# Softmax reciprocals by way of a scratch row in device memory: attention and two MLPs on one core

## The chip, the cores and the metric

The kernel runs on one core of a Trainium2 chip. The metric is the time of one execution in device microseconds. The kernel before takes 557.91 us (median of 3 runs, 557.77 to 558.45).

## What is computed

Attention over 2 batches of 8 heads, 576 tokens, head size 64, all in float32; q and k are rotated first. Two MLPs follow on the 1152 x 512 result, each 512 to 2048 to 512, with the activations h*tanh(softplus(h)) and h*sigmoid(1.702 h).

```
scores = scale * matmul(q_rot, k_rot^T);  scores -= max(scores)
attn = exp(scores);  attn = attn / (sum(attn) + 1e-9);  y = matmul(attn, v)
x = y as (1152, 512)
x = mish(x @ w_in1) @ w_out1;  out = gelu_sigmoid(x @ w_in2) @ w_out2
```

## The kernel before, in words

Work goes by pairs of heads, 8 pairs in all. For each pair the 1152 query rows (576 of each head) are cut into nine tiles of 128 rows: tile n is even for the first head and odd for the second, and tile 8 holds the last 64 rows of both heads. For every tile TensorE makes the scores (`s_mm`, L256), VectorE takes the row maximum (`s_max`, L267), ScalarE the exponential (`s_exp`, L282), which also leaves the row sums in column n of a small tile `sums`. The exponentials are turned so that keys lie on the partitions: tiles 0 to 3 as fp16 parts through a DMA transpose (`p_turn`, L368), tiles 4 to 8 on TensorE (`e_turn`, L327; `rest_turn`, L353 to L357). Then they are multiplied with v into the one bank `pvps` (`pv_mm`), in two groups: g = 0 for tiles 0 to 3 (L408, 256 columns) and g = 1 for tiles 4 to 8 (L400, 320 columns). `pv_end` (L440) multiplies the sums over v with the reciprocals `rb` and splits the result into the two parts of x.

The result of a group has head and channel on 128 partitions and queries along the row, whereas the softmax sums have queries on the partitions. The steps r_* bring the reciprocals into the first form, once for each group: ScalarE adds a small constant (`r_prep`, L374), VectorE takes the reciprocal (`r_inv`, L378), ScalarE mostly widens each of four columns to 64 (`r_wide`, at L295 in the helper `copy`), in group 1 one engine scales a 128 x 64 identity by the fifth column (`r_rest`, L384 or L386), TensorE transposes two 128 x 128 blocks, plus one matmul of 64 columns in group 1 (`r_mm`, L424 and L426), and ScalarE copies the result out of PSUM, in group 0 with the scale of v (`r_copy`, L430).

The instruction order of all engines in the attention part is written by a planner, the class `Plan`. It plays the work as a list schedule with a cost for each step, takes the ready step with the lowest rank first (table `RANK`, one number for each kind of step, plus 1 for each tile of progress), and puts tiny matmuls on idle data (`keep_clock`, L680) where its play leaves TensorE idle. Buffers limit it: the PSUM bank with tag "m" serves one step at a time, `pvps` one group at a time, and three score tiles share the rest. After the last pair, work units of the first MLP (L571) are placed between the parts of the last group of attention. SP issues loads, DMA transposes and stores in order.

The MLP part that follows runs on TensorE with weights that VectorE and ScalarE split into two parts each. The result is stored at L1143 by row tiles of 128; where the row order of attention changes within a tile, the store is cut in two.

Of the kernel before, what the change touches and what calls it, by code (L numbers as in the profile page):

```python
# [22 lines left out]
def kernel(  # L23
# [34 lines left out]
    wp = ctx.enter_context(tc.tile_pool(name="wp", bufs=3))  # L58
    stages = {}
# [21 lines left out]
    def bank(name):  # L81
        return pm.tile([128, 512], F32, tag="m", name=name)
# [19 lines left out]
    P2 = [att.tile([128, 2, 2, KB * 128], F16, name=f"p2_{i}", bufs=1) for i in range(2)]  # L102
    x = xp.tile([128, 2, KD, TOK], F32R, tag="x", name="x")
# [159 lines left out]

    def s_max(st):
# [10 lines left out]
    def s_exp(p, n, st, nm):  # L275

        if p not in sums:
            sums[p] = att.tile([128, 9], F32, tag="sums", name="sums")
        if (p, n // 2) not in ebuf:
            name, w, bufs = ("e", 2, 3) if n < 8 else ("er", 1, 1)  # L280
            ebuf[p, n // 2] = att.tile([128, w, S], F32, tag=name, name=name, bufs=bufs)
        ACT.activation(  # L282
            out=ebuf[p, n // 2][:, n % 2, :].rearrange("p (g s) -> p g s", g=2),
            in_=st[:, :, 0:HALF], func=AF.Exp,
            bias=nm, scale=SCALE, accum_out=sums[p][:, n:n + 1],
        )
# [36 lines left out]
    COL = (0, 128, 0, 192)  # L323
# [16 lines left out]
    def e_out(p, c, ps, h, eng):  # L340
        t = pt_tile(p, 1)
        if c < 4:
            copy(eng, t[:, h, :, COL[c]:COL[c] + 128], ps[:, h].rearrange("k (b q) -> k b q", b=4))
        else:
            copy(eng, t[:, :, :, 128:192], ps.rearrange("k (b h q) -> k h b q", b=4, h=2))

    def rest_turn(p):


        ps = bank("eps")  # L350
        for c in (2, 3):
            b = slice(COL[c], COL[c] + 128)
            PE.transpose(ps[:, b], ebuf[p, c][:, 1, S - 128:S], ident)  # L353
            PE.transpose(ps[0:64, b], ebuf[p, c][:, 0, MAIN:S], ident)
        e = ebuf[p, 4][:, 0]
        PE.matmul(out=ps[:, 128:192], lhsT=e[:, S - 128:S], rhs=ident[:, 64:128], start=True, stop=True)
        PE.matmul(out=ps[0:64, 128:192], lhsT=e[:, MAIN:S], rhs=ident[:, 0:64], start=True, stop=True)  # L357
        return ps[:, 0:GW[1]]
# [11 lines left out]
    def r_prep(p, g):  # L370

        n = 4 + g
        t = rcs[p, g] = att.tile([128, 16], F32, tag="rc", name="rc")
        ACT.activation(out=t[:, 0:n], in_=sums[p][:, 4 * g:4 * g + n], func=AF.Copy, bias=1e-9 * PSC)  # L374

    def r_inv(p, g):
        n, t = 4 + g, rcs[p, g]
        DVE.reciprocal(out=t[:, 8:8 + n], in_=t[:, 0:n])  # L378
        return t

    def r_rest(p, t, eng):
        rr = rrs[p, 3] = att.tile([128, 64], F32, tag="rrr", name="rrr")
        if eng is ACT:
            ACT.activation(out=rr, in_=pair_id, func=AF.Copy, scale=t[:, 12:13])  # L384
        else:
            eng.tensor_scalar(rr, pair_id, t[:, 12:13], None, op0=ALU.mult)  # L386
# [26 lines left out]
    rbs, rcs = {}, {}  # L413

    def r_wide(p, g, eng):
        rr = rrs[p, 2 * g] = att.tile([128, 4, 64], F32, tag="rr", name="rr", bufs=1)
        copy(eng, rr, rcs.pop((p, g))[:, 8:12].unsqueeze(2).to_broadcast([128, 4, 64]))

    def r_mm(p, g, ps):

        rr = rrs.pop((p, 2 * g))
        for c in range(2):
            c0 = COL[2 * g + c]
            PE.transpose(ps[:, c0:c0 + 128], rr[:, 2 * c:2 * c + 2, :].rearrange("p a d -> p (a d)"), ident)  # L424
        if g:
            PE.matmul(out=ps[:, 128:192], lhsT=block, rhs=rrs.pop((p, 3)), start=True, stop=True)  # L426

    def r_copy(p, g, ps):
        rb = rbs[p, g] = att.tile([128, GW[g]], F32, tag=f"rb{g}", name=f"rb{g}")
        ACT.activation(out=rb, in_=ps, func=AF.Copy, scale=1.0 if g else vs[p][:, 1:2])  # L430

    def pv_end(p, g):
        W, ps, rb = GW[g], pv.pop((p, g)), rbs.pop((p, g))
        del PT[p, g]
        c0 = S * (p // NPAIR) + 256 * g
# [3 lines left out]
        def norm():  # L439
            DVE.tensor_tensor(out=xf[:, 0:W], in0=ps[:, 0:W], in1=rb[:, 0:W], op=ALU.mult)  # L440
# [242 lines left out]
    class Plan:  # L683
# [6 lines left out]
            er=1, p2=2, pt0=2, pt1=2, sums=2, rc=2, rr=1, rrr=2, rb0=2, rb1=2, xf=2, vs=2, vh=2,  # L690
# [167 lines left out]
        "xl": 7061.6, "rr ACT": 8301.4, "rr DVE": 6481.1, "rr": 5509.1, "rope": 8017.6, "rope POOL": 5814.7,  # L858
        "turn": 5193.8, "load w": 6242.4, "w": 9567.2, "w POOL": 7235.3, "u": 5436.8,
# [59 lines left out]
    def plan_pair(p):  # L919
# [33 lines left out]
        for at, n in enumerate(TILES[p]):  # L953
# [41 lines left out]
            holds=[("rawv", p // 2), ("vh", p)])  # L995
        for gr in range(2):
            t = base + 4 * gr
            k = 2 * p + gr
            add("ACT", 0.095, (t, "rc"), lambda gr=gr: r_prep(p, gr),
                needs=[("e", p, c) for c in ((0, 1), (2, 3, 4))[gr]], makes=("rs", p, gr),  # L1000
                holds=[("sums", p), ("rc", k)])
            add("DVE", 0.105, (t, "rc"), lambda gr=gr: d.update({("rc", gr): r_inv(p, gr)}),
                needs=[("rs", p, gr)], makes=("rc", p, gr), holds=[("rc", k)])
            add(None, dict(ACT=0.305, DVE=0.33, POOL=0.6), (t, "rw"), lambda eng, gr=gr: r_wide(p, gr, eng),
                needs=[("rc", p, gr)], makes=("rw", p, gr), holds=[("rc", k), ("rr", k)])
            if gr:
                add(None, dict(POOL=0.4, ACT=0.24, DVE=0.12), (t, "rr"), lambda eng: r_rest(p, d["rc", 1], eng),
                    needs=[("rc", p, gr)], makes=("rr", p, gr), holds=[("rc", k), ("rrr", p)])

            def spread(gr=gr):  # L1010
                d["r", gr] = bank("rps")[:, 0:GW[gr]]
                r_mm(p, gr, d["r", gr])
            where = ("m", ("r", k))
            add("PE", 0.216 + 0.31 * gr, (t, "rm"), spread, needs=[("rw", p, gr), (("vs", p), ("rr", p, gr))[gr]], makes=("rm", p, gr),
                holds=[where, ("rr", k)] + [("rrr", p)] * gr, work=256 + 64 * gr)
            add("ACT", 0.356 + 0.053 * gr, (t, "rb"), lambda gr=gr: r_copy(p, gr, d["r", gr]),
                needs=[("rm", p, gr)], makes=("rb", p, gr), holds=[where, (f"rb{gr}", p)] + [("vs", p // 2)] * (1 - gr))
# [8 lines left out]
            def norm(gr=gr):  # L1026
                d["end", gr] = pv_end(p, gr)
                d["end", gr][0]()
            add("DVE", 0.335 + 0.067 * gr, (t, "xf"), norm, needs=[("pv", p, gr, i), ("rb", p, gr)], makes=("xf", p, gr),
                holds=[("pv", k + 1), (f"rb{gr}", p), ("xf", k)])  # L1030
# [17 lines left out]
    for t in raw_v:  # L1048
        POOL.memset(t[64:128, :, :, 4, :], 1e-27)
    for t in P2:  # L1050
        DVE.memset(t[..., S:KB * 128], 0.0)
# [139 lines left out]
```

## Time and profile before

| | |
|---|---|
| median of 3 runs | 557.91 us |
| profiled execution | 558.24 us, span 556.5 us |
| TensorE matmul busy | 548.4 us (99%) |
| TensorE weight load busy | 495.6 us (89%) |
| VectorE busy | 342.6 us (62%) |
| ScalarE busy | 266.6 us (48%) |
| GpSimd busy | 83.6 us (15%) |
| granted TensorE clock | full in all slices |

The shares are means over two unlike parts: attention up to about 150 us and the MLPs behind it. Matmuls overlap each other, and their ends are modelled, so the matmul row of TensorE shows time in which it had matmuls under way. The chain of waits follows the work that ended last back to the start; the windows view gives busy time by stage.

### The profile page before, as it was taken

To read this page: it belongs to the slowest core of one execution; us is meant where nothing else is said; L and a number is where in the kernel's file an instruction comes from. 1 tells how busy PE (TensorE), PEld (TensorE's weight loads), DVE (VectorE), ACT (ScalarE), POOL (GpSimd) and SP (SyncE) were. 2 spreads that over 40 slices of the span, in tenths; PEclk is the share of its full clock that TensorE was granted. 3 is DMA by queue.
4 is the path that set the end of the run, shared out by engine and by line. 5 is a ranking of instruction groups with operands and counts; after the bars stand their busy time and mean duration, and the time that the engine had idled before them with its cause. 6 is when DMAs were issued, how large, how long until landed. Compare 5 with 4: busy or idle time off the path is not lost.

```text
span 556.5 us, 9033 instructions
## 1 busy us (share of the span) xinstructions
PE 548.4 (99%) x3571; PEld 495.6 (89%) x3571; DVE 342.6 (62%) x691; ACT 266.6 (48%) x578; POOL 83.6 (15%) x83
## 2 busy tenths in 40 slices
PE   8999999999999999999999999999999999999996
PEld 7887777777779999999999999999988889998885
DVE  6898989899718875355886557766520437820020
ACT  2887888988618651222865122275511226741000
POOL 2696775442200000000000000000000000000000
PEclk9999999999999999999999999999999999999999
DMA  7666585653504435134433322423220124200032
GB/s 210 141 134 133 125 199 113 93 128 88 136 1 139 132 109 152 40 116 121 141 118 111 114 75 77 122 73 109 78 74 0 45 82 140 76 1 1 0 114 57
DMA packets 81034, 54.52 MB, mean 98 GB/s; under 512 B 46816, under 2 KB 77792, under 8 KB 80992
## 3 DMA queue, kind: packets, MB, share of 16 engines
q1 hardware_dynamic: 80704, 53.62, 36.3%
q8 instruction: 28, 0.46, 0.4%
q10 hardware_dynamic: 288, 0.33, 0.2%
q14 instruction: 14, 0.11, 0.1%
HBM read 41.09 MB, written 2.36 MB: 78 GB/s over the span
## 4 chain that ended last, share of the span: by engine, by line
PE 95%; DVE 3%; DMA 1%; issue 1%; SPq 0%; DVEq 0%
PE h L571 32%; PE acc L638 16%; PE acc L652 16%; PE st L256 7%; PE pvps L400 5%; PE pvps L571 4%; PE st L327 2%; PE pvps L408 2%; PE pvps L638 2%; PE tps L227 2%; PE pvps L652 2%; DVE spill L267 1%; PE rps L424 1%; PE pvps L680 1%; DMA rest<-in_k_dram 1%; PE eps L327 1%
## 5 line engine op out<-in xcount | busy, mean ns | idle before, releaser
L571 PE MATMUL h<-x,whl 128*128 128x384 f32 x1008 | 179.2, 335 | 0.0
L571 PEld LDWEIGHTS h<-x,whl 128*128 128x128 f32 x1008 | 174.9, 188 | 2.7 <-issue 2.5
L502 DVE TENSOR_TENSOR whl<-wf,whl 128x512 fp32r<-128x512 f32 x62 | 42.9, 691 | 96.1 <-ACT whl L501 96.1
L652 PE MATMUL acc<-whl,g 128*128 128x512 f32 x384 | 88.9, 389 | 0.0
L638 PE MATMUL acc<-g,whl 128*128 128x384 f32 x504 | 88.6, 334 | 0.0
L638 PEld LDWEIGHTS acc<-g,whl 128*128 128x128 f32 x504 | 87.5, 188 | 0.0
L652 PEld LDWEIGHTS acc<-whl,g 128*128 128x128 f32 x384 | 72.0, 188 | 14.9
L608 DVE TENSOR_TENSOR g<-t,g 128x384 fp32r<-128x384 f32 x96 | 53.0, 553 | 27.2 <-ACT g L618 27.2
L501 ACT ACTIVATE whl<-wf 128x512 fp32r<-128x512 f32 x64 | 40.2, 628 | 60.1 <-DVE wf L520 40.8
L267 DVE CUSTOM_DVE_ANT_1 spill<-st,shift 128x576 f16<-128x576 f32 x72 | 54.2, 753 | 9.3 <-PE st L256 4.8
L617 ACT ACTIVATE t<-h 128x384 f32<-128x384 f32 x84 | 40.5, 483 | 37.5 <-PE h L571 37.5
L618 ACT ACTIVATE g<-t 128x384 fp32r<-128x384 f32 x96 | 50.6, 527 | 3.1
L282 ACT ACTIVATE e<-st,nm 128x576 f32<-128x576 f32 x64 | 47.2, 739 | 8.2 <-DVE nm L267 7.6
L517 DVE SCALAR_TENSOR_TENSOR wf<-wraw,wf 128x512 int32<-128x512 int32 x64 | 44.1, 689 | 1.6
L520 DVE SCALAR_TENSOR_TENSOR wf<-wraw,wf 128x512 int32<-128x512 int32 x64 | 44.1, 689 | 1.3
L256 PE MATMUL st<-qk 64*128 64x288 f32 (+1 forms) x432 | 42.7, 309 | 0.0
L256 PEld LDWEIGHTS st<-qk 64*128 64x128 f32 (+1 forms) x432 | 33.8, 185 | 9.0 <-issue 5.5
L301 POOL TENSOR_TENSOR p<-e,p 128x576 f16<-128x576 f32 x26 | 34.3, 1332 | 14.6 <-DVE p L297 10.5
L1132 DVE TENSOR_TENSOR acc<-acc,acc 128x512 f32<-128x512 f32 x8 | 5.5, 687 | 37.1 <-PE acc L652 37.1
L571 PE MATMUL pvps<-x,whl 128*128 128x384 f32 x144 | 27.2, 334 | 0.0
L514 DVE TENSOR_SCALAR wf<-wraw 128x512 int32<-128x512 int32 x64 | 26.9, 420 | 0.0
L571 PEld LDWEIGHTS pvps<-x,whl 128*128 128x128 f32 x144 | 25.2, 188 | 0.0
(117 smaller groups left out, 534.6 us busy)
## 6 DMA issues: line engine op xcount, KB each, us to landing
wraw<-in_moe_w_in_dram SPq DMA_DIRECT2D x32, 512.0 KB, 3.7
wraw<-in_moe_w_out_dram SPq DMA_DIRECT2D x32, 512.0 KB, 3.5
raw_v<-in_v_dram SPq DMA_DIRECT2D x4, 512.0 KB, 6.2
raw<-in_q_dram SPq DMA_DIRECT2D x3, 512.0 KB, 3.9
raw<-in_k_dram SPq DMA_DIRECT2D x3, 512.0 KB, 5.6
out_dram<-acc SPq DMA_DIRECT2D x10, 128.0 KB, 2.4
out_dram<-acc SPq DMA_DIRECT2D x4, 256.0 KB, 2.4
raw<-in_q_dram SPq DMA_DIRECT2D x2, 256.0 KB, 3.7
```

What stands on the lines that cost most here:

```text
L256: PE.matmul(out=st[:, g, 0:HALF], lhsT=t[r, ql, c0:c0 + 128], rhs=t[r, kl, KC + HALF * g:KC + HALF * g + HALF], start=(i == 0), stop=(i == 2),
L267: DVE.tensor_tensor_reduce(out=spill, in0=st[:, :, 0:HALF], in1=shift[:, 0:1].unsqueeze(2).to_broadcast([128, 2, HALF]), scale=-SCALE, sca ...
L282: ACT.activation(out=ebuf[p, n // 2][:, n % 2, :].rearrange("p (g s) -> p g s", g=2), in_=st[:, :, 0:HALF], func=AF.Exp, bias=nm, scale=SC ...
L502: lambda: self.eng.tensor_tensor(out=t[:, 1], in0=r, in1=f32(t[:, 0]), op=ALU.subtract),
L517: lambda: DVE.scalar_tensor_tensor(out=t, in0=hi, scalar=-0x40000000, in1=t, op0=ALU.bitwise_and, op1=ALU.bitwise_or),
L520: lambda: DVE.scalar_tensor_tensor(out=t, in0=lo, scalar=29, in1=t, op0=ALU.logical_shift_right, op1=ALU.bitwise_or),
L571: PE.matmul(out=ps[:, 0:UN], lhsT=w[:, wl, 128 * kk:128 * kk + 128], rhs=src[:, xl, kk, cols(u)], start=(kk == 0 and (wl, xl) == X_LAST[0] ...
L608: DVE.tensor_tensor(out=gl, in0=t, in1=f32(gh), op=ALU.subtract)
L617: ACT.activation(out=t, in_=ps, func=func)
L618: ACT.activation(out=gh, in_=t, func=AF.Copy)
L638: PE.matmul(out=ps[:, 0:UN], lhsT=w[:, wl, 128 * f:128 * f + 128], rhs=g[:, gl, 4 * half + f, cols(u)], start=(half == 0 and f == 0 and (w ...
L652: PE.matmul(out=ps, lhsT=g[:, gl, f, 128 * t:128 * t + 128], rhs=w[:, wl, :], start=(f == 0 and (gl, wl) == TERMS[0]), stop=(f == FC - 1 a ...
```

## The change

The reciprocals of all nine tiles of a pair are made at once, when the last tile of the pair is done. `s_exp` writes the sums in the order 0, 2, 4, 6, 8, 1, 3, 5, 7. VectorE adds the constant and multiplies with the scale of v in one operation (`unit_of`, two small copies of it for each two pairs), takes nine reciprocals, and TensorE turns the 128 x 9 tile once to 9 x 128. ScalarE or VectorE copies that to SBUF, SP stores it in a row of a scratch tensor in device memory in two DMAs, and loads it back in two, each spread over 64 partitions, as `rb` of 128 x 576. Both groups of the pair take their part of that one tile. The last 64 queries move from the middle to the end of group 1's columns, and with them the cuts of the final stores. The planner gets the new steps and a new rank table, and so writes a new order.

```diff
+    unit_of = [att.tile([128, 2, 5], F32, name=f"unit_of{i}", bufs=1) for i in range(2)]
+    scratch = hbm.tile([NP, 10 * 128], F32, name="scratch")
...
+        for j in range(2):
+            DVE.tensor_copy(unit_of[j][:, :, 0:2], t[:, 0:1].unsqueeze(1).to_broadcast([128, 2, 2]))
...
-    COL = (0, 128, 0, 192)
+    COL = (0, 128, 0, 128)
...
-    def r_prep(p, g):
...
+    def r_inv(p):
+        t = rcs[p] = att.tile([128, 10], F32, tag="rc", name="rc")
+        unit = unit_of[p % 2].rearrange("p h c -> p (h c)")
+        DVE.scalar_tensor_tensor(
+            out=t[:, 0:9], in0=sums[p], scalar=1e-9 * PSC, in1=unit[:, 0:9], op0=ALU.add, op1=ALU.mult
+        )
+        DVE.reciprocal(out=t[:, 0:9], in_=t[:, 0:9])
+    def r_turn(p):
+        ps = bank("rps")[0:9, 0:128]
+        PE.transpose(ps, rcs.pop(p)[:, 0:9], ident)
+        return ps
+    def r_copy(p, ps, eng):
+        t = rts[p] = att.tile([9, 128], F32, tag="rt", name="rt")
+        copy(eng, t, ps)
+    def r_put(p, late):
+        if late:
+            SP.dma_start(out=scratch[p:p + 1, 1152:1216], in_=rts[p][4:5, 64:128])
+        else:
+            SP.dma_start(out=scratch[p, 0:1152].rearrange("(n c) -> n c", n=9), in_=rts[p])
+    def r_get(p, h):
+        if p not in rbs:
+            rbs[p] = att.tile([128, S], F32, tag="rb", name="rb")
+        src = scratch[p:p + 1, 640 * h:640 * h + S].to_broadcast([64, S])
+        SP.dma_start(out=rbs[p][64 * h:64 * h + 64], in_=src)
...
-    def r_wide(p, g, eng):
-    def r_mm(p, g, ps):
-    def r_copy(p, g, ps):
...
+        add("DVE", 0.21, (base + 4, "rc"), lambda: r_inv(p), needs=[("vs", p)] + [("e", p, c) for c in range(5)], ...
+        add("PE", 0.11, (base + 4, "rm"), lambda: d.update({"r": r_turn(p)}), needs=[("rc", p)], ...
+        add(None, dict(ACT=0.2, DVE=0.2), (base + 4, "rb"), lambda eng: r_copy(p, d["r"], eng), ...
+        for i in range(2):
+            add("SP", 0.5, (base + 4, "r put"), lambda i=i: r_put(p, i), needs=[("rt", p)], ... move=0.05, lead=1.2)
+        for i in range(2):
+            add("SP", 0.5, (base + 4, "r get"), lambda i=i: r_get(p, i), needs=[("rw", p)], ... move=0.5, lead=1.2)
...
-            k0, k1, c = next(x for x in ((0, 128, 0), (128, 256, 1), (256, 384, 2), (384, 448, None), (448, S, 3))
+            k0, k1, c = next(x for x in ((0, 128, 0), (128, 256, 1), (256, 384, 2), (384, MAIN, 3), (MAIN, S, None))
```

All numbers of `RANK` differ as well.

## Rows read from the trace of the kernel before

**Rows 1.** The page's head and its engines: busy time, share of span, instructions.
```profile
span 556.5 us, 9033 instructions
PE 548.4 (99%) x3571; PEld 495.6 (89%) x3571; DVE 342.6 (62%) x691; ACT 266.6 (48%) x578; POOL 83.6 (15%) x83
```
**Rows 2.** Busy time by stage: length, PE, PEld, DVE, ACT, POOL, granted clock, DMA share, GB/s.
```profile
0.00:33.00 33.00, 30.39 (x283) 27.05 (x284) 25.59 (x64) 19.93 (x47) 18.17 (x26) 1.00 0.67 168
...
33.00:150.00 117.00, 115.71 (x1112) 87.21 (x1109) 105.44 (x250) 97.14 (x241) 65.43 (x58) 1.00 0.61 127
...
200.00:300.00 100.00, 100.00 (x579) 100.00 (x578) 62.94 (x111) 41.50 (x82) 0.00 (x0) 1.00 0.38 116
```
**Rows 3.** Timeline of PE, the last run of idle matmuls: start, duration, instruction.
```profile
32.34 1.00 PE L680 MATMUL pvps<-idle 128*128 128x192 f16 x10
```
**Rows 4.** The chain of waits inside attention: start, time, step.
```profile
82.17 0.37 PE rps L424 x2
82.54 0.17 PE rps L426 x2
82.71 0.88 PE st L327 x8
...
91.22 0.37 PE rps L424 x2
...
145.81 0.26 PE eps L353
```
**Rows 5.** Groups by line and form, ScalarE up to 165 us: busy, mean ns.
```profile
L295 ACT ACTIVATE rr<-rc 128x256 f32<-128x256 f32 x15 | 6.2, 412 | 5.3 <-DVE rc L378 5.3
...
L430 ACT ACTIVATE rb<-rps,vs 128x256 f32<-128x256 f32 x8 | 3.8, 473 | 0.6 <-PE rps L424 0.6
L430 ACT ACTIVATE rb<-rps 128x320 f32<-128x320 f32 x8 | 3.5, 435 | 1.1 <-PE rps L426 1.1
...
L374 ACT ACTIVATE rc<-sums 128x5 f32<-128x5 f32 x8 | 1.7, 212 | 0.0
L374 ACT ACTIVATE rc<-sums 128x4 f32<-128x4 f32 x8 | 1.6, 202 | 0.0
```
**Rows 6.** Groups by line and form, VectorE up to 165 us.
```profile
L297 DVE COPY pt<-st 128x512 f32<-128x512 f32 x24 | 15.6, 684 | 0.9 <-ACT pt L295 0.9
...
L378 DVE RECIPROCAL rc<-rc 128x5 f32<-128x5 f32 x8 | 1.5, 184 | 0.2
...
L386 DVE TENSOR_SCALAR rrr<-pair_id,rc 128x64 f32<-128x64 f32 x1 | 0.2, 249 | 0.0
```
**Rows 7.** Timeline of ScalarE, L374 of group 1, first and last of eight.
```profile
30.39 0.21 ACT L374 ACTIVATE rc<-sums 128x5 f32<-128x5 f32 x1
...
145.95 0.21 ACT L374 ACTIVATE rc<-sums 128x5 f32<-128x5 f32 x1
```
**Rows 8.** Timeline of VectorE, L440 of group 0, first and last of eight.
```profile
41.62 0.42 DVE L440 TENSOR_TENSOR xf<-pvps,rb 128x256 f32<-128x256 f32 x1
...
151.12 0.42 DVE L440 TENSOR_TENSOR xf<-pvps,rb 128x256 f32<-128x256 f32 x1
```
**Rows 9.** DMA issues: count, KB each, median us from issue to landing.
```profile
out_dram<-acc SPq DMA_DIRECT2D x10, 128.0 KB, 2.4
...
pt<-p SPq DMA_TRANSPOSE x16, 4.9
rsin<-in_rope_dram ACTq DMA_DIRECT2D x1, 160.0 KB, 3.0
```
**Rows 10.** Timeline of SP: a pair's transposes, the last stores but one, the last store.
```profile
37.23 7.69 SPq L368 DMA_TRANSPOSE pt<-p  x2
...
547.66 1.11 SPq L1143 DMA_DIRECT2D out_dram<-acc  x2
...
553.10 0.34 SPq L1143 DMA_DIRECT2D out_dram<-acc  x1
```
**Rows 11.** The chain of waits, the last part of the last pair's group 1.
```profile
162.73 0.69 PE pvps L400 x4
```

More of the change, by code (lines that the diff above doesn't have):

```diff
@@ L262, in s_tile @@
         return pss.tile([128, 2, 512], F32, tag="s", name="st")
+    SUM = [5 * (n % 2) + n // 2 for n in range(9)]
     def s_max(st):
@@ L284, in s_exp @@
             in_=st[:, :, 0:HALF], func=AF.Exp,
-            bias=nm, scale=SCALE, accum_out=sums[p][:, n:n + 1],
+            bias=nm, scale=SCALE, accum_out=sums[p][:, SUM[n]:SUM[n] + 1],
         )
@@ L355, in rest_turn @@
         e = ebuf[p, 4][:, 0]
-        PE.matmul(out=ps[:, 128:192], lhsT=e[:, S - 128:S], rhs=ident[:, 64:128], start=True, stop=True)
-        PE.matmul(out=ps[0:64, 128:192], lhsT=e[:, MAIN:S], rhs=ident[:, 0:64], start=True, stop=True)
+        PE.matmul(out=ps[:, 256:320], lhsT=e[:, S - 128:S], rhs=ident[:, 64:128], start=True, stop=True)
+        PE.matmul(out=ps[0:64, 256:320], lhsT=e[:, MAIN:S], rhs=ident[:, 0:64], start=True, stop=True)
         return ps[:, 0:GW[1]]
@@ L368, in p_turn @@
         SP.dma_start_transpose(out=to, in_=t[:, both(hs)].rearrange("p a h c -> p (a h c)"))
-    def r_prep(p, g):
[L372 to L384, printed above, removed]
-        else:
-            eng.tensor_scalar(rr, pair_id, t[:, 12:13], None, op0=ALU.mult)
+    rcs, rts, rbs = {}, {}, {}
+    def r_inv(p):
[15 more added lines that the diff above has]
+            SP.dma_start(out=scratch[p:p + 1, 1152:1216], in_=rts[p][4:5, 64:128])
+        else:
+            SP.dma_start(out=scratch[p, 0:1152].rearrange("(n c) -> n c", n=9), in_=rts[p])
[4 more added lines that the diff above has]
+        SP.dma_start(out=rbs[p][64 * h:64 * h + 64], in_=src)
     pv = {}
@@ L411, in pv_mm @@
                 )
-    rbs, rcs = {}, {}
-    def r_wide(p, g, eng):
-        rr = rrs[p, 2 * g] = att.tile([128, 4, 64], F32, tag="rr", name="rr", bufs=1)
-        copy(eng, rr, rcs.pop((p, g))[:, 8:12].unsqueeze(2).to_broadcast([128, 4, 64]))
-    def r_mm(p, g, ps):
[L421 to L426, printed above, removed]
-    def r_copy(p, g, ps):
-        rb = rbs[p, g] = att.tile([128, GW[g]], F32, tag=f"rb{g}", name=f"rb{g}")
-        ACT.activation(out=rb, in_=ps, func=AF.Copy, scale=1.0 if g else vs[p][:, 1:2])
     def pv_end(p, g):
-        W, ps, rb = GW[g], pv.pop((p, g)), rbs.pop((p, g))
+        W, ps, r0 = GW[g], pv.pop((p, g)), 256 * g
+        rb = rbs[p][:, r0:r0 + W]
         del PT[p, g]
-        c0 = S * (p // NPAIR) + 256 * g
+        c0 = S * (p // NPAIR) + r0
         xh, xl = (x[:, hl, p % NPAIR, c0:c0 + W] for hl in range(2))
@@ L995, in plan_pair @@
             holds=[("rawv", p // 2), ("vh", p)])
+        add("DVE", 0.21, (base + 4, "rc"), lambda: r_inv(p), needs=[("vs", p)] + [("e", p, c) for c in range(5)],
+            makes=("rc", p), holds=[("sums", p), ("rc", p), ("vs", p // 2)])
+        add("PE", 0.11, (base + 4, "rm"), lambda: d.update({"r": r_turn(p)}), needs=[("rc", p)], makes=("rm", p),
+            holds=[("m", ("r", p)), ("rc", p)], work=128)
+        add(None, dict(ACT=0.2, DVE=0.2), (base + 4, "rb"), lambda eng: r_copy(p, d["r"], eng), needs=[("rm", p)],
+            makes=("rt", p), holds=[("m", ("r", p)), ("rt", p)])
+        for i in range(2):
+            add("SP", 0.5, (base + 4, "r put"), lambda i=i: r_put(p, i), needs=[("rt", p)], makes=("rw", p),
+                holds=[("rt", p)], move=0.05, lead=1.2)
+        for i in range(2):
+            add("SP", 0.5, (base + 4, "r get"), lambda i=i: r_get(p, i), needs=[("rw", p)], makes=("rb", p),
+                holds=[("rb", p)], move=0.5, lead=1.2)
         for gr in range(2):
@@ L998, in plan_pair @@
             k = 2 * p + gr
[L999 to L1017, printed above, removed]
             cuts = PV_CUTS[gr]
@@ L1049 @@
         POOL.memset(t[64:128, :, :, 4, :], 1e-27)
+    for t in unit_of:
+        POOL.memset(t, 1.0)
     for t in P2:
```

25 lines of the change are left out of this document (13 added, 12 removed), and 6 rows, old and new, of the table RANK.

## The prediction

> **What bounds the kernel now.** I read the page's head first: the span of the profiled execution is 556.5 us, its time 558.24, so 1.7 us lie around the span; TensorE has matmuls under way for 99% of it [rows 1]. A share over the whole span mixes attention with the MLPs, so the next view is the busy time by stage [rows 2]. From 200 to 300 us TensorE and its weight load are both at 100.00 of 100: the MLP part is a plain stream of matmuls that the change doesn't touch, and it moves as a block when attention ends earlier. From 0 to 33 us no engine is full (VectorE 25.59 of 33) and TensorE's 30.39 contain idle matmuls; the last run of these starts at 32.34 [rows 3]. Behind it, from 33 to 150 us, TensorE has 115.71 of 117, with no idle matmul among them, VectorE 105.44, ScalarE 97.14 [rows 2]. What ends last there is told by the chain of waits: around 82 and 91 us it goes from one TensorE step straight to the next, and the steps that spread the reciprocals (L424, L426) are links of it [rows 4]. So each microsecond of TensorE taken out between 33 and 150 us should bring the MLPs forward by as much, as long as no other engine takes its place.
>
> A rule of the Trainium skill speaks against that reading (Perfetto Trace Analysis, Identifying the Most-Contended Engine): matmul busy share is no good measure for TensorE, and the share of weight loading is to be taken instead. By it TensorE has only 87.21 of 117, VectorE's 105.44 comes first, and relief of TensorE is worth nothing. I go by the chain of waits, in which TensorE waits for nobody around these steps; the other reading has its chance as the second rival.
>
> **TensorE, removed.** A pair's group 1 has two transposes and a 64-column matmul: 0.37 + 0.17 = 0.54 us of the chain; its group 0 has two transposes, 0.37 [rows 4]. The first pair's group 0 runs before 33 us, among idle matmuls, and gives nothing. 8 x 0.54 + 7 x 0.37 = 6.91 us.
>
> **TensorE, added.** One transpose of a 128 x 9 block for each pair, alone in its place. The nearest row is a lone 128-column transpose, 0.26 us in the chain; the cheapest per-matmul link is half of the pair's 0.17 [rows 4], or 0.09, the dearest the pair of transposes, 0.37. I take 0.26: 8 x 0.26 = 2.08 (0.7 to 3.0). Net 4.83 us less (3.9 to 6.2).
>
> **ScalarE.** Gone for each pair: 0.202 + 0.212 for the constant, about 2 x 0.412 for widening, 0.473 + 0.435 for the copies out of PSUM [rows 5], 2.1 us in all, 17 us over the run. With 97.14 of 117 it wasn't the bound, so I count this as nothing by itself; it is room for copies that VectorE does now.
>
> **VectorE.** Two reciprocals of 0.184 [rows 6] go; one of nine columns, one constant-and-scale on nine columns and, for each two pairs, two copies of four columns come, each about 0.184 by the same row: 3 x 0.184 - 2 x 0.184, about 0.2 us more per pair. Should it also copy the 9 x 128 tile, its 64-column operation at 0.249 is the nearest row [rows 6], 0.45 us in all. A pair takes (145.95 - 30.39) / 7 = 16.5 us [rows 7]. VectorE is busy 105.44 / 117 of that, 14.9 us, and waits 1.6. TensorE's new pair would be 16.5 - 0.65 = 15.85. VectorE at 15.1 to 15.35 still fits under it, tightly. One copy of 512 columns handed to ScalarE takes 0.684 off it [rows 6] and more than pays for the growth; ScalarE's 2.1 us have the room. I count zero; bounds 0.7 us less and 0.45 more per pair.
>
> **The new wait: store, then load.** VectorE multiplies by `rb` in order, so a late `rb` would hold the row maxima queued behind it, and through them ScalarE and TensorE. From the last exponential: constant, reciprocal, transpose and copy, 0.18 + 0.18 + 0.26 + 0.25 plus hand-overs, some 1.3 us by my estimate. Two issues on SP take 1.11 [rows 10] and a store lands 2.4 after issue [rows 9]: 3.5. Two more issues and a load of 160 KB at 3.0 (each of these is 147 KB): 4.1. About 9 us in all; 13.9 if both loads queue behind a DMA transpose's 4.9 [rows 9]. Now the use: group 0 of the first pair is multiplied at 41.62, 11.2 us after the pair's last sums at 30.39 [rows 7, 8]; the six pairs behind it, by the same two views, leave 12.7 to 21.0. Only the last pair leaves little, 151.12 - 145.95 = 5.2. For seven pairs the DMA path therefore hides behind the lag that the order has anyway. For the last, group 0's end moves some 4 us back, and the five parts of group 1 with it. But these stand between work units of the first MLP that run until the last part at 162.73 [rows 11], and TensorE can do units first and parts later at the same sum. Zero, up to 3 us if the new order puts a part too early.
>
> **SP's queue.** Loads wait there for the stores to land, so for about 3 us nothing else is issued. Behind stand the next pair's DMA transposes. These start about 7 us after the pair's last sums (37.23 after 30.39) and hold SP 7.69 us [rows 7, 10]; store and load issues are through by 1.3 + 3.5 + 1.1, some 6 us. It fits, and a group 0 that the transposes feed is finished only 11 us or more after its own pair's last sums, so a small delay has room. Zero.
>
> **The end.** The last row tile of 128 was stored by one DMA; with the new cuts it spans two row orders and takes two. The last store's issue took 0.34 us, two such in a row 1.11 [rows 10]; they land 2.4 us later all the same [rows 9]. So 0.77 us more, behind everything (bounds 0 and 0.8).
>
> **The sum.** 558.24 - 4.83 + 0.77 = 554.2 in the terms of the profiled execution. That one stands 0.33 above the median of 557.91, so I predict 553.8 us, 0.7% less. Its own range, from the bounds of transpose, tail and VectorE, is 552.0 to 556.5.
>
> **Rival 1: the front shrinks too (about 550.8).** Before 33 us the order is held up by VectorE, ScalarE and GpSimd hand-overs, not by TensorE. ScalarE's relief could let it start earlier: of the 33 - 25.59 = 7.4 us in which VectorE waits, 3 more would go. For it: first-pair steps of 0.4 us each vanish from ScalarE. Against: ScalarE has 19.93 of 33 there and isn't full [rows 2].
>
> **Rival 2: VectorE becomes the bound (about 561.5).** If the new order leaves all copies where they are and VectorE keeps its 1.6 us of waits for each pair, a pair takes 14.9 + 0.45 + 1.6 = 16.95 us instead of 16.5: 7 x 0.45 = 3.2 us more, with the tail 4 us slower, 561.9 (561.5 by the median). It decides as soon as VectorE's work and waits exceed 15.85 us a pair, and there is no gain left at 16.4. For it: 90% busy, and a rank table that is wholly new, so waits can appear anywhere. Against: the chain around L424 and L426 names TensorE alone. The Trainium skill's rule above would have this outcome.
>
> **Rival 3: what TensorE saves comes back as waits (about 557.9).** The same, half way: waits of 0.6 us a pair take what the transposes leave. TensorE stood 1.3 us from 33 to 150 us, so the old order fits the chip closely; a new one need not.
>
> **Chances.** Forecast 0.62, rival 1 0.12, rival 2 0.17, rival 3 0.09. A measurement of this kernel can tell 0.2%, 1.1 us, from no change. Faster than 556.8: 0.62 + 0.12, less a little of the forecast's upper edge, 0.73; within 1.1 us: 0.09 with that edge, 0.09; slower: rival 2 with some of rival 3, 0.18. The range takes in most of rival 1 and the milder half of rival 2: 550.6 to 560.
>
> **What would show it.** Right: a single short transpose per pair on `rps` with some 0.26 us in the chain; TensorE still over 98% busy after the idle matmuls end; the first work unit of the MLP near 145.2 instead of 150; group 0's L440 never waiting for a DMA, except the last pair's; ScalarE about 16 us less; two stores after the last sum and some 0.8 us more behind it. Wrong: L440 released by the loads, VectorE idle before it, TensorE waiting for row maxima, or idle matmuls behind 33 us.

## The result, and the profile after

The changed kernel takes 561.13 us (median of 4 runs, 560.97 to 561.73), the one before 558.0 in the same comparison (557.77 to 558.45): ratio 1.006, interval 1.0048 to 1.0073. It is 3.1 us slower; the forecast was 4.1 us faster. The profiled execution took 560.98 us.

The head of the page after, against [rows 1]:

```profile
span 558.9 us, 8999 instructions
PE 546.2 (98%) x3525; PEld 489.9 (88%) x3525; DVE 346.4 (62%) x687; ACT 256.6 (46%) x541; POOL 89.7 (16%) x86
```

TensorE really has 2.2 us less under way and ScalarE 10.0 us less, and yet the span is 2.4 us longer. The busy time by stage after (columns as in [rows 2]):

```profile
0.00:33.00 33.00, 27.72 (x255) 23.86 (x255) 27.52 (x59) 17.22 (x38) 20.23 (x28) 1.00 0.77 171
33.00:150.00 117.00, 114.19 (x1069) 83.59 (x1071) 105.05 (x249) 89.95 (x214) 69.51 (x59) 1.00 0.68 140
200.00:300.00 100.00, 100.00 (x579) 100.00 (x578) 62.67 (x111) 41.91 (x82) 0.00 (x0) 1.00 0.38 116
```

The MLP stage is as before. In the attention stage TensorE now stands still for 117 - 114.19 = 2.8 us instead of 1.3. VectorE and ScalarE aren't busier there (VectorE 105.05 where it had 105.44); GpSimd has 4.1 us more, and ahead of 33 us VectorE has 1.9 more. On TensorE, then, the loss isn't work: it has less of it, and waits. The waits from 20 to 150 us that grew (engine, its line, what it waited for: us in total, times, longest), first the kernel before, then after:

```profile
ACT e L282 <- DVE nm L267: 6.5, 11, 1.5
PEld st L256 <- ACT e L282: 2.5, 7, 0.5
```

```profile
ACT e L289 <- DVE nm L274: 8.3, 13, 2.2
PEld st L261 <- ACT e L289: 7.8, 17, 1.0
ACT rt L302 <- PE rps L390: 6.0, 5, 1.8
PEld eps L360 <- ACT rt L302: 2.8, 5, 0.8
PEld pvps L421 <- DMA rb<-scratch: 0.5, 1, 0.5
```

TensorE waits three times as long as before for an exponential (7.8 against 2.5), that is, for a score buffer to come free, and the exponentials wait longer for row maxima from VectorE. The loads of `rb` hold nobody up but once, for 0.5 us. What is new on VectorE shows in the groups by line and form up to 167 us (busy, mean ns of one | idle before):

```profile
L383 DVE SCALAR_TENSOR_TENSOR rc<-sums,unit_of 128x9 f32<-128x9 f32 x8 | 4.0, 498 | 0.0
L158 DVE COPY unit_of<-vs 128x4 f32<-128x4 f32 x8 | 2.7, 385 | 0.1
L386 DVE RECIPROCAL rc<-rc 128x9 f32<-128x9 f32 x8 | 1.7, 216 | 0.3
```

Three kinds of tiny operations, which the prediction all put at 0.184 us. The reciprocal costs 0.216 every time. The other two don't have one duration; the views of their tiles give the least, the median and the greatest (ns):

```profile
L383 DVE SCALAR_TENSOR_TENSOR rc<-sums,unit_of x8: 157/532/905, 31.3 to 145.7; 128x9 f32<-128x9 f32 x8
L386 DVE RECIPROCAL rc<-rc x8: 215/216/217, 32.3 to 145.9; 128x9 f32<-128x9 f32 x8
L158 DVE COPY unit_of<-vs x8: 156/178/1322, 19.4 to 125.5; 128x4 f32<-128x4 f32 x8
```

The timeline says what decides. VectorE and GpSimd around four of these operations (start, duration):

```profile
30.92 1.28 POOL L190 TENSOR_TENSOR rtmp<-raw,rsin 128x512 f32<-128x512 f32 x1
31.33 0.91 DVE L383 SCALAR_TENSOR_TENSOR rc<-sums,unit_of 128x9 f32<-128x9 f32 x1
32.17 1.26 POOL L204 TENSOR_TENSOR rest<-rest,rsin 128x512 f32<-128x512 f32 x1
32.27 0.21 DVE L386 RECIPROCAL rc<-rc 128x9 f32<-128x9 f32 x1
...
43.27 1.62 DVE L158 COPY unit_of<-vs 128x4 f32<-128x4 f32 x2
43.58 1.28 POOL L208 TENSOR_TENSOR rest<-rest,rcos 128x512 f32<-128x512 f32 x1
...
47.53 1.27 POOL L190 TENSOR_TENSOR rtmp<-raw,rsin 128x512 f32<-128x512 f32 x1
48.26 0.57 DVE L383 SCALAR_TENSOR_TENSOR rc<-sums,unit_of 128x9 f32<-128x9 f32 x1
...
113.36 0.16 DVE L383 SCALAR_TENSOR_TENSOR rc<-sums,unit_of 128x9 f32<-128x9 f32 x1
```

L383 ends at 32.24 and at 48.83, and the GpSimd operation that ran when it started ends at 32.20 and 48.80. The second of two copies ends at 44.89, the GpSimd operation at 44.86. At 113.36 GpSimd stands idle and the same L383 takes 0.16. The reciprocal at 32.27 runs in the middle of a GpSimd operation and isn't held up. Over the whole trace five of the eight L383 start under a running GpSimd operation; each ends 0.02 to 0.04 us behind one and takes 0.49 to 0.91; the other three take 0.16. Of the eight copies at L158 three end in the same way right behind a GpSimd operation (0.39, 0.52 and 1.32); the other five take 0.16 to 0.19, one of them though GpSimd's L165 had started 0.01 us ahead of it.

The row maxima are queued behind these operations. The first work unit of the MLP starts at 150.58 after, at 150.00 before, where 145.2 was forecast (chains of waits, before and after):

```profile
150.00 2.28 PE h L571 x12
```

```profile
49.13 0.69 PE pvps L421 x4
49.81 0.21 PE rps L390
50.02 0.69 PE pvps L421 x4
...
150.58 2.28 PE h L574 x12
152.87 0.67 PE pvps L429 x10
...
167.34 0.43 PE pvps L683 x5
```

These starts are 0.6 us apart, and the spans 2.4. Behind the first work unit after has more left to do: ten matmuls of the last pair's group 0 (L429, 0.67 us), which before had done by then, five idle matmuls of the planner (L683, 0.43 us), and an end that is 0.5 us longer (4.6 us from the last sum's start to the end of the span, 4.1 before).

The lone transpose itself, between two parts of the product with v, is a link of 0.21 us, near the forecast.

### The profile page after: what moved, and what is told of

Its sections match the earlier page's. It is cut to its first block, busy times and chain, and to the rows that moved or that the text cites. A ratio compares the mean times of both kernels' runs of the same rounds, so it can differ in the third digit from the quotient of the medians.

```text
span 558.9 us, 8999 instructions
## 1 busy us (share of the span) xinstructions
PE 546.2 (98%) x3525; PEld 489.9 (88%) x3525; DVE 346.4 (62%) x687; ACT 256.6 (46%) x541; POOL 89.7 (16%) x86
## 4 chain that ended last, share of the span: by engine, by line
PE 87%; DVE 8%; DMA 2%; issue 1%; ACT 1%; SPq 0%; DVEq 0%; ACTq 0%
PE h L574 32%; PE acc L641 16%; PE acc L655 16%; PE st L261 5%; PE pvps L574 4%; PE pvps L421 3%; DVE spill L274 3%; PE pvps L429 2%; PE pvps L641 2%; PE pvps L655 2%; PE st L334 2%; PE tps L232 1%; DMA raw_v<-in_v_dram 1%; DMA rest<-in_k_dram 1%; DVE pt L304 1%
## 5 line engine op out<-in xcount | busy, mean ns | idle before, releaser
L505 DVE TENSOR_TENSOR whl<-wf,whl 128x512 fp32r<-128x512 f32 x64 | 44.7, 699 | 94.9 <-ACT whl L504 94.9
L261 PE MATMUL st<-qk 64*128 64x288 f32 (+1 forms) x432 | 44.6, 311 | 1.8 <-ACT e L289 1.7
L308 POOL TENSOR_TENSOR p<-e,p 128x576 f16<-128x576 f32 x29 | 38.5, 1345 | 31.5 <-DVE p L304 22.5
```

Of the source, the lines that this page charges most:

```text
L261: PE.matmul(out=st[:, g, 0:HALF], lhsT=t[r, ql, c0:c0 + 128], rhs=t[r, kl, KC + HALF * g:KC + HALF * g + HALF], start=(i == 0), stop=(i == 2),
L505: lambda: self.eng.tensor_tensor(out=t[:, 1], in0=r, in1=f32(t[:, 0]), op=ALU.subtract),
```

## The experiments

The runs were timed in four groups, each beside the kernel before on the same chip (557.6 to 557.83 us there). By the intervals the difference of two runs is good to some 0.7 to 0.9 us. "Before" and "after" name the two kernels of the case.

**Steps or order?** The first two runs take the steps r_* out of either order, everything else in its place.

```diff
 # e1, in before: r_prep, r_inv, r_rest, r_wide, r_mm, r_copy
+        pass
-        W, ps, rb = GW[g], pv.pop((p, g)), rbs.pop((p, g))
+        W, ps, rb = GW[g], pv.pop((p, g)), fixed
```

> The kernel before, in its own order, with all reciprocal steps left out (the division by the softmax sums is missing, a constant tile stands for rb). It tests the main term of the prediction: TensorE bounds attention, so its 6.9 us of spreading come out of the time whole. If that holds: 558.0 - 6.9 = 551.1 us (550 to 552.5). If VectorE bounds attention (rival 2 of the prediction), whose share of the removed steps is only 3 us in all: 556 to 558.

Measured: 555.79 us against 557.75, ratio 0.996 (0.9948 to 0.9972). Taking away *all* of the old steps brings 2.0 us, less than a third of the 6.91 that the prediction counted for their TensorE part alone.

```diff
 # e2, in after: r_inv, r_turn, r_copy, r_put, r_get, and the copies into unit_of
+        pass
-        rb = rbs[p][:, r0:r0 + W]
+        rb = fixed[:, 0:W]
```

> The changed kernel, in its own order, with its reciprocal steps left out in the same way. What is left is the same attention work as in the first run, only in the new order and with the new cut of the stores. Theory A (the new operations cost: constant-and-scale and the copies of the scale wait on VectorE while GpSimd works, 4 us more than their work): it falls to the first run's time plus 0.5 for the stores, about 551.6 if that is 551.1. Theory B (the new order loses TensorE time whatever the new operations cost): it stays well above the first run, by 4 us or more, 555.5 to 559.

Measured: 555.93 us, ratio 0.9969 (0.996 to 0.9978). The two orders without the steps are 0.14 us apart, less than can be told: the new order with its store cuts isn't clearly worse, and it is the new steps that cost 561.13 - 555.93 = 5.2 us where the old cost 2.0.

**What of the new steps?** e3 keeps the order, the transposes and the DMAs, and changes only how the scale of v gets in: one reciprocal straight from the sums (without the tiny constant), and the scale, a different one for the rows of group 0 and 1, as a 9 x 1 operand of the copy out of PSUM.

```diff
-            DVE.tensor_copy(unit_of[j][:, :, 0:2], t[:, 0:1].unsqueeze(1).to_broadcast([128, 2, 2]))
+        DVE.tensor_scalar(unit_of[p // 2 % 2], pick[:, 0:1], t[0:9, 1:2], pick[:, 1:2], op0=ALU.mult, op1=ALU.add)
...
-        DVE.scalar_tensor_tensor(
-            out=t[:, 0:9], in0=sums[p], scalar=1e-9 * PSC, in1=unit[:, 0:9], op0=ALU.add, op1=ALU.mult
-        )
-        DVE.reciprocal(out=t[:, 0:9], in_=t[:, 0:9])
+        DVE.reciprocal(out=t[:, 0:9], in_=sums[p])
...
-        copy(eng, t, ps)
+            ACT.activation(out=t, in_=ps, func=AF.Copy, scale=unit_of[p // 2 % 2])
```

> The changed kernel in its own order, with a cheaper preparation: one reciprocal straight from the sums (the constant of 1e-9 is dropped), and the scale of v as a scalar of each partition in the copy out of PSUM; one tensor_scalar of 9 x 1 for each two pairs in place of two copies of 128 x 4. VectorE is rid of 4.0 us (L383) and 2.7 us (L158). Theory A: 557 us (556 to 558), 3 to 5 less than the changed kernel's 561.1. Theory B: 560 to 561.

Measured: 557.98 us against 557.75, ratio 1.0004 (0.9995 to 1.0012). Level with before: 3.15 us of the 5.2 come back. Its groups of lines show what VectorE does now:

```profile
L382 DVE RECIPROCAL rc<-sums 128x9 f32<-128x9 f32 x8 | 1.6, 205 | 0.0
L158 DVE TENSOR_SCALAR unit_of<-pick,vs 9x1 f32<-9x1 f32 x4 | 1.0, 243 | 0.0
```

The start of the first operation on `rc`, pair by pair, tells where after falls behind e3: by 0.85, 1.78, 1.98, 1.99, 2.83, 2.47, 2.66 and 2.66 us. It grows in three places, not evenly. The first lies ahead of the first L383. There the scale's two copies, right behind the reciprocal that they copy, put VectorE's next big operation 0.37 us behind that reciprocal's start; in e3, with one operation, it is 0.25. GpSimd's L165 is released by the same reciprocal and starts 0.26 behind it in both. The timelines of after and of e3 at this step:

```profile
19.17 0.16 DVE L156 RECIPROCAL vs<-vs 128x1 f32<-128x1 f32 x1
19.36 0.26 DVE L158 COPY unit_of<-vs 128x4 f32<-128x4 f32 x2
19.43 0.80 POOL L165 TENSOR_SCALAR vh<-raw_v,vs 128x640 f16<-128x640 f32 x1 [2.99 <-DVE vs L156]
19.54 1.29 DVE L308 TENSOR_TENSOR p<-e,p 128x576 f16<-128x576 f32 x1
```

```profile
19.49 0.16 DVE L157 RECIPROCAL vs<-vs 128x1 f32<-128x1 f32 x1
19.57 0.24 DVE L158 TENSOR_SCALAR unit_of<-pick,vs 9x1 f32<-9x1 f32 x1
19.74 0.74 DVE L308 TENSOR_TENSOR p<-e,p 128x576 f16<-128x576 f32 x1
19.75 1.76 POOL L165 TENSOR_SCALAR vh<-raw_v,vs 128x640 f16<-128x640 f32 x1 [2.98 <-DVE vs L157]
```

In after GpSimd is first, and VectorE's L308 takes 1.29; in e3 VectorE is first by 0.01 us, L308 takes 0.74, and it is GpSimd's L165 that takes 1.76 instead of 0.80. The same happens once more, with the two engines' L190 at 26.8 us (after, then e3):

```profile
26.77 1.28 POOL L190 TENSOR_TENSOR rtmp<-raw,rsin 128x512 f32<-128x512 f32 x1
26.87 1.73 DVE L190 TENSOR_TENSOR rtmp<-raw,rsin 128x512 f32<-128x512 f32 x1
```

```profile
26.59 0.68 DVE L190 TENSOR_TENSOR rtmp<-raw,rsin 128x512 f32<-128x512 f32 x1
26.66 1.75 POOL L190 TENSOR_TENSOR rtmp<-raw,rsin 128x512 f32<-128x512 f32 x1
```

The second place holds L383 at 31.33 and the copy at 43.56 (1.32 us); the third is the stretch from 81 to 98 us. L383 at 64.31, which took 0.85, cost nothing: the next pair is no further behind. That these places are the cause is read from where the lag grows; no run took them one by one.

**The copies by themselves.** e5 is after with the scale taken by a reciprocal instead of the copy:

```diff
-            DVE.tensor_copy(unit_of[j][:, :, 0:2], t[:, 0:1].unsqueeze(1).to_broadcast([128, 2, 2]))
+            DVE.reciprocal(out=unit_of[j][:, :, 0:2], in_=t[:, 1:2].unsqueeze(1).to_broadcast([128, 2, 2]))
```

> The changed kernel with one edit: the two small copies of the scale (L158, 2.7 us on VectorE for eight, one pair of them 1.62) become reciprocals of the same size, which have the same result and took 0.16 to 0.22 us each time in both traces. Theory A1 (of the 3.1 us that the port-free kernel won, most is the constant-and-scale, 4.0 us on VectorE): 560 to 560.5. Theory A2 (the copies, which come when the front is tight, are most of it): 558.5 to 559.

Measured: 560.04 us, ratio 1.0045 (1.0032 to 1.0058): by the medians the copies are worth 1.1 us, which leaves some 2.05 for L383. The intervals of e5 and after (1.0048 to 1.0073) overlap, so this split is rough. In e5's trace the eight reciprocals at L158 take 0.148 to 0.161 us, none of them held up, but L383 now takes 0.159 to 1.035, with a median of 0.670 against 0.532 in after.

**Is it VectorE's time or its wait for GpSimd?** e8 is e3 with 24 reciprocals more, three behind each that is there:

```diff
-        DVE.reciprocal(out=t[:, 0:9], in_=sums[p])
+        for _ in range(4):
+            DVE.reciprocal(out=t[:, 0:9], in_=sums[p])
```

> The port-free kernel with each reciprocal of 128 x 9 done four times over: 24 more of 0.2 us, 4.9 us more on VectorE, none of which has to wait for GpSimd. The changed kernel had 5.7 us more on VectorE than the port-free one and took 3.15 us longer, 0.55 for each. If VectorE's time is the price, whatever it goes by: 558.0 + 2.7 = 560.7. If only waits in which GpSimd holds VectorE count: 558 to 558.8.

Measured: 559.27 us, ratio 1.0027 (1.0018 to 1.0036), 1.3 us above e3. The group shows what was added, 6.8 - 1.6 = 5.2 us:

```profile
L383 DVE RECIPROCAL rc<-sums 128x9 f32<-128x9 f32 x32 | 6.8, 213 | 0.8
```

5.2 us that wait for nobody cost 1.3, or 0.25 for each. From e3 to after VectorE's new operations grow by 8.4 - 2.9 = 5.5 us (4.0 + 2.7 + 1.7 against 1.6 + 1.0 and one copy of 0.3), and that costs 3.15, or 0.57 for each. At e8's price 5.5 us would cost some 1.4 of the 3.15, an estimate, since e8's operations stand at one of the places only. The rest, by this reckoning, is where the waits fall and what they shift.

**TensorE.** e6 is e1 with the 40 spreading matmuls of before put back, on constant tiles, so that nobody waits for them:

```diff
-            PE.transpose(ps[:, c0:c0 + 128], rr[:, 2 * c:2 * c + 2, :].rearrange("p a d -> p (a d)"), ident)
+            PE.transpose(ps[:, c0:c0 + 128], block, ident)
```

> The kernel before without its reciprocal steps (555.8), with TensorE's 40 transposes and spreading matmuls put back, on constant tiles that nobody has to make or copy; the division is missing. Left out are only ScalarE's, VectorE's and GpSimd's parts. If TensorE bounds attention, as the prediction had it, all of the 2.0 us between 555.8 and 557.75 come back: 557.8. If the other engines' parts were the price: 555.8 to 556.3.

Measured: 558.12 us, ratio 1.0006 (0.9997 to 1.0015), 2.3 above e1. The matmuls account for all that the old steps cost; beside them ScalarE's 17 us and VectorE's reciprocals cost nothing that the measurement can tell.

e11 puts the eight lone transposes into e2, on a constant tile; e10 puts only the reciprocals there, e12 both, the transposes then waiting for them.

```diff
 # e11
-        pass
+        ps = bank("rps")[0:9, 0:128]
+        PE.transpose(ps, pair_id[:, 0:9], ident)
```

> The changed kernel's order without reciprocal steps (555.9), with only the eight reciprocals of 128 x 9 on VectorE put back (their result is not used, the division is missing): 1.7 us of VectorE. At the price of the padding run, 0.26 for each: 556.3. C1: 556 to 556.4. C2 with VectorE as the cause: 557 or more.

> The same kernel (555.9) with only the eight transposes of 128 x 9 put back, on a constant tile, so that they wait for nobody and nobody copies them (the division is missing). Forty matmuls cost 2.3 us in the order before, 0.06 each; eight at that price: 556.4. By the prediction's price of 0.26: 558.0. C1: 556 to 556.5.

> The same kernel (555.9) with reciprocals and transposes put back as in the port-free kernel, the one waiting for the other, but no copy out of PSUM, so that nothing holds the bank (the division is missing). C1: 556.3 to 557, and the rest up to 558.0 comes with the copy. C2, if it is the wait of the transpose for VectorE: 557.5 to 558.

Measured: e10 556.2 us (0.9973; 0.9963 to 0.9983), e11 557.81 (0.9996; 0.9987 to 1.0005), e12 557.72 (1.0001; 0.9992 to 1.001). Over e2's 555.93 that is 0.3, 1.9 and 1.8: each lone transpose costs 1.88 / 8 = 0.235 us of the whole time (good to some 0.1), and the wait for the reciprocal nothing that can be told. Eight such cost nearly as much as the old forty in e6, 2.3 / 40 = 0.06 each. That isn't a price of the matmuls: from the start of each to the start of the next matmul, TensorE spends 1.47 us on the eight in e11, 0.18 each, and 6.35 us on the forty in before and in e6, 0.16 each. Without the forty, about 4 of those 6.35 us come back elsewhere, as the question on TensorE further below shows.

**The bank.** In e3 TensorE's L360 waits for the copy of `rt`, since one PSUM bank serves both steps in turn:

```profile
ACT rt L392 <- PE rps L386: 6.4, 5, 1.9
PEld eps L360 <- ACT rt L392: 3.0, 6, 0.6
```

e9 gives both steps different columns of one bank, so that L360 needs no copy before it.

```diff
-        ps = bank("rps")[0:9, 0:128]
+        if p not in shared:
+            shared[p] = bank("eps")
+        ps = shared[p][0:9, 384:512]
```

> The port-free kernel (558.0) with the turned reciprocals in the last 128 columns of the bank into which the rest of the pair's exponentials is turned anyway, so that this turn (L360) no longer waits until ScalarE has copied the reciprocals out. In the changed kernel TensorE's loader stood 2.8 us in five such waits. Theory C1 (this hand-over is most of the 2.05 us left over the kernel without reciprocals, 555.9): 556.5 to 557. Rival C2 (it is VectorE's reciprocal or the transpose itself): 557.6 to 558.2.

Measured: 558.28 us, ratio 1.0013 (1.0 to 1.0027), nothing gained. The wait stays in the trace, with the lines moved by three (L363 is e3's L360):

```profile
PEld eps L363 <- ACT rt L397: 3.0, 6, 0.6
```

So the edit didn't remove the wait, and what the wait is worth stays open; e12, which has no such copy, only shows that copy, DMAs and this wait together come to 0.26 us between e12 and e3, no more than the measurement can tell.

**The DMA path.** e7 is e3 without stores and loads, `rb` from a constant.

```diff
 # e7: r_put and r_get
+        pass
```

> The port-free kernel (558.0) without the two stores and two loads of each pair; a constant tile stands for rb, so the division is missing. If the way through device memory is hidden, as the prediction had it: 557.7 to 558.2. If the wait for the stores on SP or the late load of the last pair is what is left over the kernel without reciprocals (555.9): 556 to 556.5.

Measured: 558.04 us, ratio 1.0007 (0.9997 to 1.0016). Nothing, within some 0.7 us: the way through device memory is hidden. In after the loads land 3.2 us behind their issue:

```profile
rb<-scratch SPq DMA_DIRECT2D x16, 144.0 KB, 3.2
```

**The end.** e4 is after with the old cuts of the final stores.

```diff
-            k0, k1, c = next(x for x in ((0, 128, 0), (128, 256, 1), (256, 384, 2), (384, MAIN, 3), (MAIN, S, None))
+            k0, k1, c = next(x for x in ((0, 128, 0), (128, 256, 1), (256, 384, 2), (384, 448, None), (448, S, 3))
```

> The changed kernel with the old cut of the final stores, so that the last row tile is stored by one DMA (the last rows of each batch land in the wrong rows of the output). Only the end changes: 0.5 us less by the two traces (from the last sum's start to the end of the span 4.1 us before, 4.6 after), 560.6; if the second store costs nothing, 561.1.

Measured: 560.81 us, ratio 1.0051 (1.0038 to 1.0063), 0.3 us less than after; the intervals overlap, so the size rests on the two traces' 0.5.

**Why did 7 us of TensorE bring only 2?** In e1 the wait of the exponentials for row maxima takes over, and TensorE waits for score buffers (the same two rows as in the section before):

```profile
ACT e L283 <- DVE nm L268: 17.1, 21, 1.8
PEld st L257 <- ACT e L283: 4.7, 13, 0.6
```

17.1 us against 6.5, and 4.7 against 2.5. On TensorE one can see where the saving went. From the start of each matmul to the start of the next, the 384 score matmuls of 288 columns on 64 rows (`st` from `qk`, L256) take 32.65 us in before and 35.97 in e1; the transposes into `st` and `eps` take another 1.0 us more. The removed matmuls had taken 6.35, so about 4 of these come back as time in which TensorE stands at the scores and the turns of the exponentials. In e6, with the matmuls put back, the scores take 32.47 again. The chain of waits moves with it. By its pieces from 33 to 147 us, VectorE and ScalarE have 5.6 us of it in before and 21.5 in e1. A theory was that TensorE and VectorE are so evenly loaded that either alone brings little and both together much. e13 is before with VectorE relieved at one line (the low part of v set to zero: that correction is left out), e14 is e1 with the same. 5.6 us less was expected; in e13's trace the line takes 2.6 us where it took 7.0, so the relief is 4.4.

```diff
-        DVE.scalar_tensor_tensor(
-            out=t[:, 1], in0=v_of(p)[:, p % 2], scalar=vs[p][:, 0:1], in1=t[:, 0], op0=ALU.mult, op1=ALU.subtract
-        )
+        DVE.memset(t[:, 1], 0.0)
```

> The kernel before with the low part of v set to zero by a memset in place of computed (L164, 0.88 us for each pair on VectorE; the correction by that part is missing): some 5.6 us less on VectorE, nothing else changed. It is one corner of a square with the kernel without reciprocal steps (2.0 us less) and the next run. If TensorE bounds the old order by itself: 557.3 to 557.7. If VectorE does: about 553. If the two hold each other, as the runs so far suggest: 556 to 557.

> The kernel before without its reciprocal steps (555.8) and with the light low part of v as well. If what TensorE was spared there came back as waits for VectorE, relief of both brings more than the two reliefs one by one: less than 555.8 minus the gain of the run beside it, 552.5 to 553.5. If the lost 4.6 us had another cause (the order itself, the transfers): no more than the sum of the two, 554.5 or more.

Measured: e13 557.02 us against 557.83, ratio 0.9985 (0.9976 to 0.9993); e14 555.88, ratio 0.9967 (0.9956 to 0.9978). The theory falls: with both relieved, the time is that of e1 alone. The wait of the exponentials from 33 to 147 us is the same in e1 and in e14, in sum, number and longest:

```profile
ACT e L283 <- DVE nm L268: 14.4, 17, 1.8
```

```profile
ACT e L281 <- DVE nm L266: 14.4, 17, 1.8
```

So VectorE's sum of work doesn't hold the 555.8. The rows point to the round from scores to maximum to exponential to the next free score buffer, in the order in which the planner has put it; no run here changed that round alone, so this is read from the waits and not shown. In the next runs, another order brings the scores back to 32.74 us (e16).

**A version from what was learned.** e15 and e16 are e3 with the transpose as a ninth matmul of `rest_turn`, in its bank, where it needs no place of its own, the second half of the last store on ScalarE's queue, and two rank tables written for it.

```diff
+        PE.transpose(ps[0:9, 384:512], rcs.pop(p)[:, 0:9], ident)
+        return ps[:, 0:GW[1]], ps[0:9, 384:512]
...
-            SP.dma_start(out=rows[j - k0:j - k0 + n, :], in_=acc2[r:r + n, t, :])
+            (ACT if t == NT - 1 and r else SP).dma_start(out=rows[j - k0:j - k0 + n, :], in_=acc2[r:r + n, t, :])
```

> A version meant to be better: the port-free kernel with the transpose of the reciprocals as the ninth matmul of the pair's last turn on TensorE (L360 to L364), not between parts of the product with v; the second of the two last stores goes out on ScalarE's queue; the planner knows the new steps and has a rank table of its own. Eight lone transposes cost 1.9 us; as neighbours of transposes 0.11 each by the chain: 1.0 less, the store 0.3 less. 556.7 if the new order is worth the others, 555.5 to 558.5 for what an order can do.

> The same with another rank table, to see how far orders of nearly the same planned length (155.9 and 156.2 us in the planner's own play) lie apart on the chip: 556.7, 555.5 to 558.5; the two within 1 us of each other.

Measured: e15 558.02 us, ratio 1.0006 (0.9993 to 1.0019); e16 557.15, ratio 0.9982 (0.9969 to 0.9994). e16 is the only one that leaves no work out beyond the tiny constant and beats before, by 0.2%; the two differ in nothing but the rank table, so what lies between them, 0.9 us by the medians and about what can be told, is the order's. The transposes didn't get cheaper by their new place: from start to next start they take 1.57 us in e16's trace, 0.20 each, against 0.18 alone.

The granted TensorE clock belongs to this comparison. Six of e16's twelve executions show a mean of 0.995 to 0.997 and took 557.04 to 558.75 us; the six at 0.998 to 1.0 took 555.6 to 557.28, median 556.1, which is 1.7 below before. Of the 35 executions of before one lies under 0.998. No kept trace of e16 shows where its clock falls; e2's profiled execution (mean 0.995) shows such a fall, to 0.50 from 18 to 20 us, the lower of the clock's two levels, behind a stretch from 14 to 18 us in which TensorE had matmuls under way for 2.81 us of 4. So e16's order gains more than its median says, and loses it again in half of its executions.

## Why the prediction was wrong

The difference of 561.13 - 557.75 = 3.38 us, from the medians above. Each step is good to some 0.7 to 0.9 us, so the three small ones can't be told from nothing, and the table names no cause by itself:

| step | us | from |
|---|---|---|
| old steps gone | -1.96 | e1 |
| new order and store cuts, without the steps | +0.14 | e2 - e1 |
| eight lone transposes | +1.88 | e11 - e2 |
| reciprocals and the wait for them | -0.09 | e12 - e11 |
| copy out of PSUM, stores, loads | +0.26 | e3 - e12 |
| constant-and-scale and the copies of the scale | +3.15 | after - e3 |

**"TensorE, removed" failed: 6.91 forecast, 2.0 measured (2.3 for the matmuls alone, e6).** The durations were nearly right: the forty matmuls take 6.35 us in before, from start to next start. The error is to price the removal of a step by its link in the chain of waits. The chain tells through which steps the time ran. It doesn't tell how close behind them the next chain lies, and here it lay close: with the steps gone, e1's exponentials wait 17.1 us for row maxima instead of 6.5, and TensorE spends 3.3 us more on the same 384 score matmuls. In e1 the loss of 4.9 us against the forecast has the form of rival 3, the savings come back as waits. Why the round over the score buffers is no faster than that stays open; VectorE's sum of work isn't the reason (e14). The sign could have been read before: ScalarE already waited 11 times for row maxima in the kernel before, 6.5 us in all, a row that the prediction didn't look at.

The rule that the prediction weighed at that point (the Trainium skill, Perfetto Trace Analysis, Identifying the Most-Contended Engine) would have made relief of TensorE worth nothing. e1's 2.0 us lie nearer to that than to the chain's 6.91. Its other half, that VectorE as the busier engine is the bound, isn't borne out: e13 took 4.4 us from VectorE and gained 0.8.

**"VectorE" failed: zero forecast, 3.15 us measured.** The step took 0.184 us for each small operation from the reciprocal's row [rows 6] and looked only at size. Two of the three new operations were of a kind that the trace shows waiting for GpSimd: one with two inputs in SBUF, and a copy from SBUF to SBUF. Nothing in [rows 6] is a measure for them, but the trace of before had GpSimd at 65.43 of 117 us [rows 2], so that an operation of this kind has better than an even chance to meet it. The step's upper bound, 0.45 us a pair, covers what was measured, but by luck: it stood for a copy of the 9 x 128 tile. The Trainium skill has the rule (SBUF — State Buffer, Who interferes with whom): VectorE and GpSimd share a pair of SBUF ports as an exclusive lock, an operation of VectorE with two SBUF inputs, or a copy in a two-port mode, waits for it, one with a single SBUF input outside these modes doesn't. This trace agrees, with 0.157 to 0.905 us for L383 and 0.215 to 0.217 for L386, three of whose eight run under a GpSimd operation.

**"TensorE, added" came out right in size:** 0.26 forecast, 0.235 measured for each in e11, against 0.21 as a link of the chain.

**ScalarE at nothing was right**, and so were **the new wait at zero** (e7: no change; one wait of 0.5 us) and **SP's queue at zero**.

**"The end"** was too high: 0.77 forecast, 0.3 by e4 and 0.5 by the traces (4.6 us after, 4.1 before).

**"The sum"** has a range of its own, 552.0 to 556.5, which doesn't come out of its bounds: with transposes, end and VectorE at theirs it reaches up to 558.24 - 3.9 + 0.8 + 7 x 0.45 - 0.33 = 558.0. The measured 561.13 lies outside either.

**The rivals.** Rival 2's time, 561.5, came within 0.4 us, but not by its own way: it had a pair take 16.95 us instead of 16.5, and from the first L383 to the last, 31.3 to 145.7, a pair takes 16.3. VectorE's work did grow, by 3.8 us over the whole run. Rival 2 named the engine on which the loss arises, not the mechanism. Rival 3 describes what became of TensorE's saving. Rival 1 was wrong: the front doesn't shrink, and after loses its first 0.85 us against e3 in it.

**The signs.** The prediction would show itself wrong, it said, by VectorE idle before L440, or TensorE waiting for row maxima, or idle matmuls behind 33 us. The second came, by way of the exponentials, and so did the last: seven idle matmuls from 33.2 to 34.7 us and the five at 167, which are links of the chain. Of the signs of being right, TensorE had 97.6% of the stage instead of over 98, and ScalarE 10.0 us less instead of about 16; the only wait for a load of `rb` was the last pair's, as it said.

## What to carry to other kernels

Take a link in the chain of waits as an upper bound on what removing it can give (here 6.91 us of links gave 2.0); before counting it, look in the waits for the next chain behind it (here ScalarE for row maxima) and, where a run can be had, take the step out entirely. A small operation on VectorE is priced by its operands, not by its size alone: where GpSimd is busy half the time, give it one SBUF operand, as e3's reciprocal has, and leave the scale to a copy that is made anyway. The way through device memory cost nothing here, where the order leaves it 10 us or more for all pairs but the last.

## What the runs showed of the hardware

- A 128 x 9 operation with two SBUF inputs takes 0.16 us with GpSimd idle, up to 0.91 with GpSimd at work; a 128 x 4 copy 0.16 and 1.32. In the pairs of rows above the engine that starts first keeps its usual time and the other waits: the same 128 x 512 operation took 0.68 us on VectorE when it started 0.07 us ahead of GpSimd's, 1.73 when it started 0.10 behind.
- Eight lone 128 x 9 transposes and forty spreading matmuls occupy TensorE alike, 0.18 and 0.16 us from each start to the next, and yet cost 0.235 and 0.06 us of the whole time each: how much comes back depends on the order around them.
- What reaches the end of some 5 us of VectorE time differs: 1.3 of 5.2 us as reciprocals (e8), 0.8 of 4.4 when the low part of v is relieved (e13), 3.15 of 5.5 as operations that meet GpSimd.
